# Work moved from VectorE to ScalarE in the first block: normalisations, every second negative branch, two weight casts

## The chip, the core and the metric

The kernel runs on one core of a Trainium2 chip. PE is the matrix engine TensorE, DVE is VectorE, ACT is ScalarE, POOL is GpSimd and SP is SyncE, which issues the transfers. The metric is the device time of one execution in microseconds (us), as the median of several runs.

## The reference

Causal window attention with a distance bias feeds a leaky two-matrix MLP, and that feeds a second MLP. All values are fp32.

```python
scores = scale * q @ k.T                     # 4 batches, 8 heads, 576 rows, 64 wide
scores = where(0 <= rel < 128, scores + bias, -1e9)
x = softmax(scores) @ v                      # as 2304 tokens x 512
h = x @ w_in                                 # 512 x 2048
g = maximum(h, 0) + alpha * minimum(h, 0)    # alpha: one number for each of 2048 columns
x = g @ w_out                                # 2048 x 512
h = x @ w_in2
out = (h * sigmoid(1.702 * h)) @ w_out2
```

## The kernel before

**Numbers in two parts.** Most products are made of a high and a low part: a cast to the rounded type gives the high part (`wh`, `xh`, `gh`), a subtraction the low part (`wl`, `xl`, `gl`), and three matmuls stand for one exact product. The weights come as 64-bit patterns and are turned into fp32 on the chip. There are 32 chunks of 128x512 for the first MLP, two for each of 16 columns of tiles f. A chunk is loaded to `ws`; ACT scales its two halves (`w_scale`, lines 146 and 147); DVE masks the sign (line 151), shifts (156) and adds (161) into `wd`; and `w_split` casts the high part (lines 101 and 102) and subtracts for the low one (106). `HI_DVE` names the chunks whose cast is done by DVE, all others go to ACT. There are four buffers `ws`; the next load is issued when the add of the chunk four places earlier is in the program (`w_ahead`).

**Attention.** An item is one head of one batch, and the first 16 items (n below 16) take a form in full fp32. For each, PE makes scores `s` (line 342), DVE adds the bias and finds the extreme (362), ACT takes the exponential (378), DVE the reciprocal of the sum (386, 387), `a_norm` multiplies by it (396 on ACT, 398 on DVE), PE transposes to `pt` (411), ACT copies `pt` out of PSUM (418) and PE multiplies by v, held in `vz` (432). An item has two tiles here, of 128 and 256 columns. With `"mix"` the first is normalised on DVE and the second on ACT, with `"act"` both on ACT. Items from 16 on split q and k in two parts (lines 315 to 352) in buffers that take the place of the first form's.

**First MLP.** Block k is 256 tokens, which are eight items, so block 0 can start when items 0 to 7 are done. A unit (k, f) has four steps: `m1_h` makes h in one of two PSUM banks (line 493), `m1_n` makes `n = min(h, 0) * alpha` (line 507), `m1_g` makes `g = max(h, 0) + n` (513) and its high part (515), `m1_lo` the low part, and `m1_o`, two units later, accumulates the second product (537). Two units go with one item.

**Order.** A first loop runs items 0 to 9 with the decoding of about 20 chunks. Then come the units of block 0 (k = 0) with items 10 to 17 and the other chunks. The blocks from 1 on have no decoding until the last. Within this program a scheduler that works on a modelled timeline places the instructions of each engine, so that the order of one engine's queue is not that of the text. From the last block of the first MLP on the order of some instructions is pinned.

Of the kernel before, what the change touches and what calls it, by code (L numbers as in the profile page):

```python
# [11 lines left out]
F32 = mybir.dt.float32  # L12
# [3 lines left out]
AF = mybir.ActivationFunctionType  # L16
ALU = mybir.AluOpType
# [4 lines left out]
P = 128  # L22
NF = DFF // P
# [17 lines left out]
         {2: (0, 256, 0), 1: (256, 192, 0), 3: (448, 192, 128), 4: (640, 64, 256)})  # L41
MASKED = 1.0e9 * 256.0

HI_DVE = (0, 2)
NST, NWD = 4, 3
KM = NB1 - 2

# [18 lines left out]
def tile_window_attention__then__two_mlps(  # L66
# [13 lines left out]
    nc = tc.nc  # L80
    usrc = (u0, u1)

    const = ctx.enter_context(tc.tile_pool(name="const", bufs=1))
# [7 lines left out]
    ident = const.tile([P, P], F32, name="ident")  # L91
    relt = const.tile([P, 2 * P], F32, name="relt")
    alph = const.tile([P, NF], F32, name="alph")
    x2d = [dram.tile([P, NC, T1], F32, name=f"x2d{i}") for i in range(NB1)]
    g2d = [
        [dram.tile([P, 2, n], F32, name=f"g2d{j}_{p}") for p in range(NF // 2)] for j, (t, n) in enumerate(BLOCKS)
# [2 lines left out]
    def copy(eng, o, i):  # L99
        if eng == "act":  # L100
            return nc.scalar.copy(o, i)  # L101
        return (nc.vector if eng == "dve" else nc.gpsimd).tensor_copy(o, i)

    def sub(eng, o, a, hi):
        e = nc.vector if eng == "dve" else nc.gpsimd
        return e.tensor_tensor(o, a, hi.bitcast(F32), op=ALU.subtract)  # L106
# [5 lines left out]
    def pin(ins):  # L112
        if pinned:
            tc.keep_in_program_order(ins)
# [49 lines left out]
    def w_split(i):  # L164
# [14 lines left out]
        h, l = wt[layer, f]  # L179
        pin(copy("dve" if i in HI_DVE else "act", h[:, part, :], w))  # L180
        pin(sub("dve", l[:, part, :], w, h[:, part, :]))
# [38 lines left out]
    def w(step, lim=2 * NF):  # L220

        names = ("load", "scale", "sign", "shift", "add", "split")
        i = wdone.get(step, 0)
        if i < min(lim, wdone.get(names[names.index(step) - 1], 0)):
            {"scale": w_scale, "sign": w_sign, "shift": w_shift, "add": w_add, "split": w_split}[step](i)
            wdone[step] = i + 1
# [107 lines left out]
    @stage  # L334
    def a_qk(n, b, u, h, U):
        banks = [ps_a.tile([P, 2, 256], F32, tag="a", name="s") for _ in range(1 + u)]
        places = []
        for i, (c0, rows, kk, keys) in enumerate(U["chunks"]):
            o = banks[i // 2][:rows, i % 2, :]
            if n < FP:  # L340
                raw = raw_of(n)[:D]
                nc.tensor.matmul(
                    o[:, :keys], raw[:, c0 : c0 + rows], raw[:, 256 + kk : 256 + kk + keys], start=True, stop=True
                )
                places.append(o[:, :keys])
                continue
            n_ = max(keys, 192)
            kh, kl = ar["kh"], ar["kl"]
            q = ar["q"][:, c0 - U["q0"] : c0 - U["q0"] + rows]
            ks = kk - U["k0"]  # L350
            nc.tensor.matmul(o[:, :n_], q, kh[:, ks : ks + n_], start=True, stop=False)  # L351
            nc.tensor.matmul(o[:, :n_], q, kl[:, ks : ks + n_], start=False, stop=True)  # L352
            places.append(o[:, :keys])
        st["s", n] = places
# [45 lines left out]
    @stage  # L400
    def a_trans(n, b, u, h, U):
        tt = tts[n % 2]
        banks = [ps_a.tile([P, 512], F32, tag="a", name="pt") for _ in range(1 + u)]
        for i, (c0, rows, kk, keys) in enumerate(U["chunks"]):
            for j in range(kk // P, (kk + keys + P - 1) // P):
                col, nq, oc = PTCOL[u][j]
                bank = 1 if col >= 448 else 0
                dst = col - (0, 448)[bank] + (c0 - U["q0"] - oc)

                src = tt[:, i * 256 + j * P - kk : i * 256 + j * P - kk + P]  # L410
                nc.tensor.transpose(banks[bank][:, dst : dst + P], src, ident)  # L411
        st["t", n] = [(x, c, w) for x, (c, w) in zip(banks, ((0, 384), (448, 256)))]
# [45 lines left out]
    @stage  # L458
    def a_x2(n, b, u, h, U):
        nq = U["nq"]  # L460
        if n < FP:
            return
        x = st.pop(("x", n))
        d0 = (h % 2) * D
        nc.vector.tensor_tensor(xps[d0 : d0 + D, :nq], x[:D, :nq], tb[:, :nq], op=ALU.add)

    @stage
    def a_x3(n, b, u, h, U):
        if h % 2 == 0:
            return  # L470
        nq, c, xp = U["nq"], h // 2, xps
        if n < FP:
            xp = st["x", n]
        t = u * B * UNITS[0]["nq"] + b * nq
        done = 0
        while done < nq:
            r = (t + done) % RING
            w = min(nq - done, RING - r)
            nc.scalar.copy(xh[:, c, r : r + w], xp[:, done : done + w])
            sub("dve", xl[:, c, r : r + w], xp[:, done : done + w], xh[:, c, r : r + w])  # L480
            done += w


    gs, accs = {}, {}

    def m1_h(k, f):
        hi, lo = wt[0, f]
        r = (k * T1) % RING
        n = T1 if k < KM else 2 * T1
        ph = ps_h.tile([P, DM], F32, tag="h", name="h")[:, :n]  # L490
        for c in range(NC):
            for i, (w, x) in enumerate(((hi, xh), (hi, xl), (lo, xh))):
                nc.tensor.matmul(  # L493
                    ph, w[:, 0, c * P : (c + 1) * P], x[:, c, r : r + n],
                    start=(c == 0 and i == 0), stop=(c == NC - 1 and i == 2),
                )
        gs[k, f] = ph

    def m1_tile(k, pool, dt, name):
        if k < KM:  # L500
            return pool.tile([P, T1], dt, tag=name, name=name)
        return p2["n1" if name == "n" else "g1"].tile([P, 2 * T1], dt, tag=name, name=name)

    def m1_n(k, f):
        ph = gs[k, f]
        n = m1_tile(k, gt[0], F32, "n")
        nc.vector.tensor_scalar(n, ph, 0.0, alph[:, f : f + 1], op0=ALU.min, op1=ALU.mult)  # L507
        gs[k, f] = (ph, n)

# [246 lines left out]
    n = H + 2  # L756
# [6 lines left out]
    a_x1(n - 2)  # L763
    a_x2(n - 2)
    a_x3(n - 2)
    at0.close()
    gp[0] = p1.enter_context(tc.tile_pool(name="g", bufs=3, side="right"))
    gt[0] = p1.enter_context(tc.tile_pool(name="gt", bufs=2, side="right"))
# [1 line left out]
    steps = [(k, f) for k in range(KM + 1) for f in range(NF)]  # L770
    for s, (k, f) in enumerate(steps):
        n = H + 2 + s // 2
        norm = "mix" if k == 0 else "act"
        if (k, f) == (KM, 0):
            pinned.append(True)
        dec = k == 0 or k == KM
        lim = min(3 * NF, max(W1, wdone["split"]) + 3) if k else W1

        def wd(*names):
            for x in names if dec else ():  # L780
                w(x, lim)

        m = -1 if n == FP else n - 1
        m1_h(k, f)
        if s % 2 == 0:
            a_trans(m)
            a_qk(n)
            a_pt_hi(m, 0)
            m1_n(k, f)
            wd("sign")  # L790
            m1_g(k, f)
            a_pt_hi(m, 1)
            a_bias(n)
            wd("shift")
            a_pt_lo(m, 0)
            a_pt_lo(m, 1)
            wd("add", "scale")
            w_ahead()
            if n + 1 != FP:
                a_split(n + 1)  # L800
            a_exp(n)
            m1_lo(k, f, "dve")
        else:
            a_av(m)
            a_recip(n)
            a_split_v(n)
            a_load(n + 2)
            a_norm(n, norm)
            m1_n(k, f)
            wd("sign")  # L810
            m1_g(k, f)
            a_x1(n - 1)
            wd("shift", "scale")
            a_x2(n - 1)
            wd("add")
            w_ahead()
            m1_lo(k, f, "dve")
            a_x3(n - 1)
            if n + 1 == FP:
                a_trans(n)  # L820
                a_pt_hi(n, 0)
                a_av(n)
                a_parts()
                a_split(FP)
        if k == 0:
            w("split")
        m1_o(k - (f < LAG), (f - LAG) % NF)
        if n == NI + 1 and s % 2:
            at.close()
            p2["ps"] = ctx.enter_context(tc.tile_pool(name="ps_p", bufs=1, space=PSUM))  # L830
            p2["x", 0] = ctx.enter_context(tc.tile_pool(name="p20", bufs=1))
            pre = ExitStack()
            p2["g1"] = pre.enter_context(tc.tile_pool(name="g1", bufs=3))
            p2["n1"] = pre.enter_context(tc.tile_pool(name="n1", bufs=2))
            w_ahead()
        if k == KM:
            w("split", min(3 * NF, W1 + 2 * (f - 2)))
            if f >= 8 and f % 2 == 0:
                x2_split(0, f // 2 - 4)
            if f >= 6 and f % 2 == 0 and f < 14:  # L840
                x2_load(0, f // 2 - 3)
# [11 lines left out]
    ph = ExitStack()  # L853
# [105 lines left out]
```

## Time and profile before

| | |
|---|---|
| median of 3 runs | 979.54 us (978.63 to 979.56) |
| profiled execution, its own time | 976.72 us |
| its span, first to last instruction | 974.9 us |
| PE busy | 937.9 us, 96% of the span |
| DVE busy | 717.0 us, 74% |
| ACT busy | 561.1 us, 58% |
| POOL busy | 89.1 us, 9% |

The shares are means over stages that differ much: block 0 with the decoding lies in the first 131 us, the rest of the first MLP up to 715 us, the second MLP behind that. An end of a matmul in such a profile is modelled, so the distance between the starts of two matmuls is the better measure of PE's rate.

### The profile page before, as it was taken

The page shows a single profiled execution, that of the slowest core. Times are in us where ns is not written, and L with a number is a line of the kernel's source. Part 1 is how long each engine was busy: PE and PEld are TensorE (multiplying, and loading weights), DVE is VectorE, ACT ScalarE, POOL GpSimd, SP SyncE. Part 2 cuts the span into 40 slices and gives each one's busy share as a digit, 9 for nine tenths or more (in the row PEclk, how much of TensorE's full clock was granted, in tenths as well). Part 3 has the DMA queues.
Part 4 walks back from the last instruction along what each step waited for, and adds up shares of the span by engine and source line. Part 5 has one row for each costly group of instructions (what it writes and reads, how often), then busy time and mean ns, then how long its engine had stood idle before and what let it go on. Part 6 is the DMA issues. An engine that isn't in the chain of part 4 may idle for free.

```text
span 974.9 us, 17672 instructions
## 1 busy us (share of the span) xinstructions
PE 937.9 (96%) x6536; PEld 868.4 (89%) x6536; DVE 717.0 (74%) x1777; ACT 561.1 (58%) x1355; POOL 89.1 (9%) x126
## 2 busy tenths in 40 slices
PE   4889989999999999999999999999999989999997
PEld 2579989999999999999988888888888879999997
DVE  5999957778777777777667863897232798878876
ACT  5987656667877777787633443654232644334333
POOL 1000011112222222222100000000000000000000
PEclk9999999999999999999999999999999999999999
DMA  8655521212212223222022334766322333343323
GB/s 240 197 176 169 179 65 55 77 43 86 88 65 88 66 68 94 78 62 93 2 77 85 109 129 153 234 204 220 120 97 87 142 124 125 131 151 109 131 87 109
DMA packets 43894, 112.43 MB, mean 115 GB/s; under 512 B 5024, under 2 KB 15008, under 8 KB 43808
## 3 DMA queue, kind: packets, MB, share of 16 engines
q1 hardware_dynamic: 43808, 111.31, 35.7%
q8 instruction: 51, 0.84, 0.4%
q14 instruction: 35, 0.29, 0.1%
HBM read 82.98 MB, written 28.31 MB: 114 GB/s over the span
## 4 chain that ended last, share of the span: by engine, by line
PE 82%; DVE 2%; issue 1%; ACT 1%; DMA 0%; DVEq 0%; SPq 0%; ACTq 0%
PE h L583 19%; PE h L493 19%; PE p L650 17%; PE o L537 14%; PE p L537 5%; PE x L444 3%; PE pt L411 3%; PE s L351 1%; PE s L352 1%; ACT oh L101 0%; DMA wd<-x2d 0%; DVE ol L106 0%; DVE gs L624 0%; DVE wl L106 0%; DVE g L597 0%
## 5 line engine op out<-in xcount | busy, mean ns | idle before, releaser
L493 PE MATMUL h<-xh,wh 128*128 128x256 f32 (+1 forms) x512 | 154.3, 304 | 3.4 <-DVE g L513 3.3
L493 PE MATMUL h<-xl,wh 128*128 128x256 f32 (+1 forms) x512 | 157.1, 307 | 0.3 <-DVE xl L106 0.3
L493 PE MATMUL h<-xh,wl 128*128 128x256 f32 (+1 forms) x512 | 155.0, 303 | 0.0
L650 PE MATMUL p<-wh,oh 128*128 128x256 f32 x504 | 136.8, 284 | 1.7 <-ACT oh L101 1.3
L650 PE MATMUL p<-wl,oh 128*128 128x256 f32 x504 | 136.5, 283 | 0.0
L537 PE MATMUL o<-gl,wh 128*128 128x256 f32 x448 | 125.2, 281 | 0.6 <-DVE gl L106 0.6
L537 PE MATMUL o<-gh,wl 128*128 128x256 f32 x448 | 124.6, 280 | 0.0
L537 PE MATMUL o<-gh,wh 128*128 128x256 f32 x448 | 122.7, 280 | 0.0
L650 PE MATMUL p<-wh,ol 128*128 128x256 f32 x504 | 120.4, 283 | 1.9 <-DVE ol L106 1.9
L583 PE MATMUL h<-x2h,wh 128*128 128x512 f32 (+1 forms) x320 | 118.3, 370 | 2.2 <-DVE g L597 2.2
L583 PE MATMUL h<-x2l,wh 128*128 128x512 f32 (+1 forms) x320 | 117.7, 368 | 0.0
L583 PE MATMUL h<-x2h,wl 128*128 128x512 f32 (+1 forms) x320 | 117.7, 368 | 0.0
L597 DVE TENSOR_TENSOR g<-h,sg 128x512 f32<-128x512 f32 (+1 forms) x80 | 50.8, 637 | 76.7 <-ACT sg L593 76.3
L493 PEld LDWEIGHTS h<-xh,wh 128*128 128x128 f32 x512 | 98.2, 193 | 8.6 <-DVE g L513 4.1
L493 PEld LDWEIGHTS h<-xl,wh 128*128 128x128 f32 x512 | 98.6, 193 | 5.2 <-DVE st L387 1.3
L493 PEld LDWEIGHTS h<-xh,wl 128*128 128x128 f32 x512 | 98.8, 193 | 2.9
L593 ACT ACTIVATE sg<-h 128x512 f32<-128x512 f32 (+1 forms) x80 | 44.3, 555 | 98.6 <-PE h L583 98.0
L650 PEld LDWEIGHTS p<-wh,oh 128*128 128x128 f32 x504 | 96.4, 192 | 3.0 <-ACT oh L101 2.9
L507 DVE TENSOR_SCALAR n<-h,alph 128x256 f32<-128x256 f32 (+1 forms) x128 | 65.4, 513 | 43.3 <-PE h L493 42.1
L650 PEld LDWEIGHTS p<-wl,oh 128*128 128x128 f32 x504 | 96.7, 192 | 0.1
L650 PEld LDWEIGHTS p<-wh,ol 128*128 128x128 f32 x504 | 86.8, 192 | 2.7 <-DVE ol L106 2.5
L537 PEld LDWEIGHTS o<-gl,wh 128*128 128x128 f32 x448 | 84.2, 188 | 1.9 <-DVE gl L106 0.8
(105 smaller groups left out, 2234.5 us busy)
## 6 DMA issues: line engine op xcount, KB each, us to landing
ws<-in_w_in_dram SPq DMA_DIRECT2D x32, 512.0 KB, 3.6
ws<-in_w_out_dram SPq DMA_DIRECT2D x32, 512.0 KB, 3.9
raw<-in_u_dram SPq DMA_DIRECT2D x32, 512.0 KB, 3.5
g2d<-g SPq DMA_DIRECT2D x32, 512.0 KB, 3.0
gr<-g2d SPq DMA_DIRECT2D x32, 512.0 KB, 3.3
raw<-in_u_dram SPq DMA_DIRECT2D x16, 320.0 KB, 3.0
wd<-x2d SPq DMA_DIRECT2D x36, 128.0 KB, 3.2
out_dram<-ob SPq DMA_DIRECT2D x16, 256.0 KB, 3.9
```

Of the source, the lines that this page charges most:

```text
L351: nc.tensor.matmul(o[:, :n_], q, kh[:, ks : ks + n_], start=True, stop=False)
L352: nc.tensor.matmul(o[:, :n_], q, kl[:, ks : ks + n_], start=False, stop=True)
L411: nc.tensor.transpose(banks[bank][:, dst : dst + P], src, ident)
L444: nc.tensor.matmul(x[:, oc : oc + nq], v, p[:, col : col + nq], start=(i == 0 and k == 0), stop=(i == len(js) - 1 and k == 1), skip_group_ ...
L493: nc.tensor.matmul(ph, w[:, 0, c * P : (c + 1) * P], x[:, c, r : r + n], start=(c == 0 and i == 0), stop=(c == NC - 1 and i == 2),)
L507: nc.vector.tensor_scalar(n, ph, 0.0, alph[:, f : f + 1], op0=ALU.min, op1=ALU.mult)
L537: nc.tensor.matmul(o, w[:, 1, c * P : (c + 1) * P], g, start=(f == 0 and (k == KM or c % 2 == 0) and i == 0), stop=(f == NF - 1 and i == 2 ...
L583: nc.tensor.matmul(ph[:, :n], w[:, f % 2, c * P : (c + 1) * P], x[:, c, :n], start=(c == 0 and i == 0), stop=(c == NC - 1 and i == 2),)
L593: nc.scalar.activation(sg[:, :n], ph[:, :n], AF.Sigmoid, scale=1.702)
L597: nc.vector.tensor_tensor(g[:, f % 2, :n], ph[:, :n], sg[:, :n], op=ALU.mult)
L650: nc.tensor.matmul(o[:, m, :], g[:, a, m * P : (m + 1) * P], w, start=(p == 0 and m == 0 and i == 0), stop=(p == NF // 2 - 1 and i == 2), ...
```

## The change

Three things move from DVE to ACT, all of them in the first 131 us. In block 0 the negative branch n of every unit with odd f is made by ACT, in two instructions: a relu of -h, and a multiplication by -alpha, which lies in a new tile `nalph`. POOL fills that tile once. In block 0 `a_norm` puts both tiles of an item on ACT. And `HI_DVE` is empty, so that the casts of chunks 0 and 2 go to ACT as well.

```diff
-HI_DVE = (0, 2)
+HI_DVE = ()
...
+    nalph = const.tile([P, NF], F32, name="nalph")
...
     def m1_n(k, f):
         ph = gs[k, f]
         n = m1_tile(k, gt[0], F32, "n")
+        if k == 0 and f % 2:
+
+            nc.scalar.activation(n, ph, AF.Relu, scale=-1.0)
+            nc.scalar.mul(n, n, nalph[:, f : f + 1])
+            gs[k, f] = (ph, n)
+            return
         nc.vector.tensor_scalar(n, ph, 0.0, alph[:, f : f + 1], op0=ALU.min, op1=ALU.mult)
...
     a_x3(n - 2)
+    nc.gpsimd.tensor_scalar(nalph, alph, -1.0, None, op0=ALU.mult)
     at0.close()
...
-        norm = "mix" if k == 0 else "act"
+        norm = "act"
```

The scheduler gives all engines another order from there on; line numbers after the change are up to 8 higher. On DVE, at the first two units of block 0, there stand before (`n` and `g` as above, `tt` the tile of scores, `s` in PSUM):

```order
L507 TENSOR_SCALAR n<-h,alph 128x256 x2
L106 TENSOR_TENSOR wl_569<-wd,wh_568 128x512
L161 ISA wd<-ws,wd 128x1024
L362 ISA tt_145,st_147<-s,relht 128x128
L362 ISA st_147 128x1
L362 ISA tt_145,st_147<-s,relht 128x256
L362 ISA st_147 128x1
L513 SCALAR_TENSOR_TENSOR g<-h,n 128x256
```

After the change the same place on DVE reads:

```order
L514 TENSOR_SCALAR n<-h,alph 128x256
L107 TENSOR_TENSOR wl_570<-wd,wh_569 128x512
L157 SCALAR_TENSOR_TENSOR wd<-wd,ws 128x512
L520 SCALAR_TENSOR_TENSOR g<-h,n 128x256
L152 TENSOR_SCALAR ws<-ws 128x512
L363 ISA tt_146,st_148<-s,relht 128x128
L363 ISA st_148 128x1
L363 ISA tt_146,st_148<-s,relht 128x256
L363 ISA st_148 128x1
L162 ISA wd<-ws,wd 128x1024
```

One of the two n is gone, and the first g stands ahead of the bias of the item, not behind it.

On ACT the place of the second and third odd unit of block 0 reads after the change:

```order
L510 ACTIVATE n<-h 128x256
L102 CAST wh_663<-wd 128x512
L511 ACTIVATE n<-n,nalph 128x256
L147 ACTIVATE wd<-ws 128x512
L102 CAST wh_751<-wd 128x512
L522 CAST gh<-g 128x256
L397 ACTIVATE tt_146<-tt_146,st_148 128x128
L397 ACTIVATE tt_146<-tt_146,st_148 128x256
L148 ACTIVATE ws<-ws 128x512
```

Relu and scaling are parted by other work, and the two normalisations of an item follow each other. Before, the stretch around the same casts on ACT had neither n nor a normalisation of 128 columns:

```order
L515 CAST gh<-g 128x256 x2
L147 ACTIVATE ws<-ws 128x512
L146 ACTIVATE wd<-ws 128x512
L101 CAST wh_661<-wd 128x512
L396 ACTIVATE tt_145<-tt_145,st_147 128x256
L101 CAST wh_661<-wd 128x512
```

On PE, the transposes of an item of block 0 stand after the change on both sides of the next item's scores (`o` is the second product, `raw` holds q and k):

```order
L412 MATMUL pt<-ident,tt_147 128x128
L343 MATMUL s<-raw_144 128x128
L343 MATMUL s<-raw_144 128x256
L412 MATMUL pt<-ident,tt_147 128x128 x2
L544 MATMUL o_755<-gl,wh_976 128x256
```

Before, the three transposes of an item stood together, ahead of the scores:

```order
L411 MATMUL pt<-ident,tt_146 128x128 x3
L342 MATMUL s<-raw_143 128x128
L342 MATMUL s<-raw_143 128x256
L537 MATMUL o_752<-gl,wh_860 128x256
L537 MATMUL o_752<-gh,wl_861 128x256
```

The two transposes that need the second tile moved behind the scores.

## Rows read from the trace of the kernel before

**Rows 1.** Busy time by stage; columns: stretch, its length, engines, clock, DMA share, GB/s

```profile
0.00:20.00 20.00, 6.66 (x17) 4.11 (x18) 10.64 (x33) 10.77 (x25) 2.66 (x14) 1.00 0.79 233
20.00:62.00 42.00, 37.26 (x111) 25.42 (x110) 38.90 (x112) 37.47 (x91) 4.49 (x9) 1.00 0.70 210
62.00:70.30 8.30, 6.39 (x33) 5.64 (x34) 7.64 (x21) 5.77 (x15) 0.30 (x1) 0.80 0.60 168
70.30:118.00 47.70, 47.11 (x371) 44.33 (x371) 47.20 (x125) 33.89 (x77) 1.64 (x4) 1.00 0.52 163
118.00:131.00 13.00, 9.03 (x63) 7.75 (x63) 5.96 (x23) 7.21 (x22) 2.52 (x6) 1.00 0.42 129
131.00:715.00 584.00, 583.08 (x4075) 542.83 (x4075) 417.01 (x1081) 366.29 (x951) 77.53 (x92) 1.00 0.31 98
```

**Rows 2.** Order of time on PE: start, length, instruction, idle time before it

```profile
54.35 0.41 PE L493 MATMUL h<-xh,wl 128*128 128x256 f32 x1
54.56 0.41 PE L493 MATMUL h<-xl,wh 128*128 128x256 f32 x1
...
60.90 0.39 PE L493 MATMUL h<-xl,wh 128*128 128x256 f32 x1 [0.34 <-DVE xl L106]
...
61.13 0.28 PE L493 MATMUL h<-xh,wl 128*128 128x256 f32 x1
61.24 0.28 PE L493 MATMUL h<-xl,wh 128*128 128x256 f32 x1
...
62.18 0.52 PE L411 MATMUL pt<-ident,tt 128*128 128x128 f32 x3 [0.54 <-DVE tt L398]
...
64.85 0.45 PE L432 MATMUL x<-pt,vz 128*128 128x256 f32 x1 [1.30 <-ACT pt L418]
...
66.17 0.39 PE L493 MATMUL h<-xh,wh 128*128 128x256 f32 x1 [0.43 <-DVE g L513]
...
113.89 0.39 PE L537 MATMUL o<-gl,wh 128*128 128x256 f32 x1 [0.56 <-DVE gl L106]
...
127.12 0.33 PE L351 MATMUL s<-kh,q 128*128 128x192 f32 x1 [1.18 <-ACT vp L331]
...
130.73 0.39 PE L493 MATMUL h<-xh,wh 128*128 128x256 f32 x1 [1.97 <-DVE g L513]
```

**Rows 3.** Waits of PE from 58 to 131 us: total, times, longest

```profile
PE x L432 <- ACT pt L418: 2.4, 3, 1.3
...
PE h L493 <- DVE g L513: 2.4, 2, 2.0
```

**Rows 4.** Order of time on ACT, the instruction ahead of a pt copy

```profile
63.67 0.67 ACT L147 ACTIVATE ws<-ws 128x512 int32<-128x512 uint32 x1 [1.15 <-DMA ws<-in_w_out_dram]
```

**Rows 5.** Groups by form, 62 to 118 us: busy us, mean ns, idle before

```profile
L147 ACT ACTIVATE ws<-ws 128x512 int32<-128x512 uint32 x13 | 8.9, 686 | 10.0 <-DMA ws<-in_w_out_dram 5.8 <-DMA ws<-in_w_in_dram 4.2
...
L507 DVE TENSOR_SCALAR n<-h,alph 128x256 f32<-128x256 f32 x15 | 7.0, 474 | 0.0
...
L515 ACT CAST gh<-g 128x256 fp32r<-128x256 f32 x15 | 6.0, 407 | 0.0
...
L396 ACT ACTIVATE tt<-tt,st 128x256 f32<-128x256 f32 x6 | 3.1, 514 | 0.1
...
L398 DVE TENSOR_SCALAR tt<-tt,st 128x128 f32<-128x128 f32 x6 | 1.7, 277 | 0.0
```

**Rows 6.** Line 102, the casts on DVE: duration min/median/max in ns, starts

```profile
L102 DVE CAST wh<-wd x2: 420/422/423, 11.8 to 19.1; 128x512 fp32r<-128x512 f32 x2
```

**Rows 7.** Groups by form on ACT, 0 to 131 us

```profile
L101 ACT CAST wh<-wd 128x512 fp32r<-128x512 f32 x30 | 18.5, 617 | 3.6 <-DVE wd L161 3.5
...
L418 ACT COPY pt<-pt 128x384 f32<-128x384 f32 x16 | 7.5, 472 | 3.8 <-PE pt L411 3.8
...
L378 ACT ACTIVATE tt<-tt,st 128x128 f32<-128x128 f32 x17 | 6.8, 402 | 3.9 <-DVE st L362 3.7
...
L331 ACT CAST vp<-raw 128x128 fp32r<-128x128 f32 x2 | 0.6, 295 | 0.0
```

## The prediction

> **What bounds the kernel now.** I read the busy time by stage first, since the change touches only the first 131 us of a span of 974.9 us [rows 1]. From 131 us to 715 us PE is busy for 583.08 of 584.00 us: what that stretch takes is PE's work alone, and DVE and ACT with 417 and 366 us have room. Nothing the change does to their load there can matter, except through the moment at which the stretch begins. So the question is when block 0 of the first MLP ends, at about 131 us.
>
> Ahead of that three stages differ. From 20 to 62 us, the loop over the first heads, all three engines are near their limit: PE 37.26, DVE 38.90 and ACT 37.47 of 42 us. PE is that busy because it is slow: two matmuls of 256 columns start 0.21 us apart at 54 us, and 0.11 us apart at 61 us [rows 2]. That is the 1.2 GHz level first and the 2.4 GHz level then; the granted clock of the stretch reads 1.00, so for this stage I go by the starts. PE had worked nearly without gaps before it rose.
>
> From 62 to 70.3 us PE idles for 1.91 us (8.30 less 6.39) and its granted clock is 0.80 on the mean. A mean of 0.80 is 3.3 us at half speed, so 1.66 us of PE's work are lost (8.3 x 0.20). Just before it fell, PE had waited four times, and its rows say for what [rows 2]: 0.34 us for xl, 0.54 us for a normalised tile, 1.30 us for a pt copy, 0.43 us for g. In the view of waits from 58 to 131 us [rows 3] g has 2.4 us in two waits, the other of them at 130.7 us, and pt copies have 2.4 us in three. The 1.30 us look like ACT, but the row of ACT [rows 4] shows that the instruction ahead had waited 1.15 us for a weight load. That load could start only when the DVE add of an earlier chunk had freed its buffer. Here PE waits for DVE four times, once by way of a DMA and ACT.
>
> From 70.3 to 118 us PE is busy for 47.11 of 47.70 us and DVE for 47.20. Both are full; PE's one gap there is 0.56 us for gl at 113.9 us [rows 2]. ACT is busy for 33.89 us, and 10.0 us of its idle time between 62 and 118 us stand before one line, waiting for weight loads [rows 5]. From 118 to 131 us PE idles for 3.97 us: the last head of the first form, the switch of the pools, and the first units of block 1.
>
> **The change part by part.** DVE loses 8 multiplications n of 474 ns, 8 normalisations of 277 ns [rows 5] and 2 casts of 422 ns [rows 6]: 3.79 + 2.22 + 0.84 = 6.85 us, all before 131 us.
>
> ACT takes over four kinds. The two casts cost 617 ns there [rows 7], 1.23 us. They fall where DVE had them, at 11.8 and 19.1 us [rows 6], and there ACT is busy for 10.77 of 20 us [rows 1]; this cover hides the first, and the second stands at the edge of the full stage, where it costs nothing or up to 0.62 us. The normalisation of 128 columns has no row on ACT. It lies between 295 ns (a cast of that size without a per-partition operand) and 402 ns (an exponential with two) [rows 7]; I take 400, as it has one: 3.2 us. The scaling by nalph is of the form of the normalisation of 256 columns, 514 ns [rows 5]: 4.1 us. The relu reads PSUM; between the cast of 128x256, 407 ns [rows 5], and the copy of 384 columns out of PSUM, 472 ns [rows 7], I take the first: 3.3 us. In sum ACT gains 11.8 us.
>
> Is there room? From 62 to 118 us ACT is busy for about 39.7 of 56 us (5.77 + 33.89) [rows 1]. Some 7 of the 8 pairs and 6 of the normalisations fall there, 7 x 0.92 + 6 x 0.40 = 8.8 us, which makes 48.5 us or 87%. DVE goes from 54.8 to 49.9 us, 89%. No engine but PE is then full. The order of ACT has no additional table load.
>
> What PE gets. In the 47.7 us where PE is full, a faster DVE gives nothing. What can be won are PE's gaps up to 118 us. By 63 us DVE is ahead by the two casts and one n, 0.84 + 0.47 = 1.3 us. That is as much as the waits for xl, the tile and g together, which are all for DVE (0.34 + 0.54 + 0.43 = 1.31 us): they go. Of the 1.30 us behind the weight load I count half, 0.65: the load starts as much earlier as the add does, but ACT gets a relu and a scaling in the same queue. The 0.56 us for gl goes, since DVE has 5 us in hand by then. Sum 2.5 us. The 1.66 us of the clock I leave out of the sum: whether it falls depends on how the gaps lie. The bounds of this term are 0 (the gaps only move) and 4.8 us (all of 3.2 us of gaps and the clock).
>
> The gaps from 118 to 131 us stay. They are a serial chain (pt copy, the last product with v, the first q and kh of the new form, bias, g) and the order has the same chain in it; what is late next is this chain, which starts as early as PE is done.
>
> What is queued behind the new instructions: behind a relu, which waits for PE, stand on ACT weight scalings, casts wh, gh casts and the pt copy of the head. The two normalisations of a head now follow each other on ACT, so the second half of a tile is ready about 0.4 us later; the order of PE puts the scores of the next head between the first transpose and the other two. That hides it. Without that cover it would be 8 x 0.4 = 3.2 us. The single nalph instruction on POOL stands there ahead of copies of v, and POOL is busy for 4.49 of 42 us from 20 us on and 2.66 of 20 before [rows 1]. On SP only neighbours among the loads swap; the weight loads follow the DVE adds as before.
>
> The profiled execution is 976.72 us for a span of 974.9 us. The three timed runs have a median of 979.54 us, 2.8 us above it; the difference is applied to the median: 979.54 - 2.5 = 977.0 us. A change of 0.2%, 1.96 us, is about what can be told from none.
>
> **The rivals.** *Nothing reaches PE.* The gaps before 70 us belong to the slow, full stage before them, in which PE itself at 1.2 GHz is the pace. DVE then idles where it was full. For it: PE has no gap at all for most of 47.7 us. Against: three of the four waits before 66.2 us name DVE [rows 2]. Time: 979.5 us, between 978 and 981.
>
> *ACT becomes late.* For an odd unit, h now goes through two ACT instructions, 0.92 us in place of 0.47, and through a queue with 87% load. PE's bank of h is free that much later. If PE had no other matmul to run, each of the 8 units would cost 0.45 us, 3.6 us in all: 983.1 us. It decides from the point where an odd unit's g is later than the 12 matmuls that follow its h, 12 x 0.115 = 1.4 us at the spacing of 61 us [rows 2]. For it: PE waits as long for pt copies as for g [rows 3]. Against: ACT's 10 us of waits for loads [rows 5], which the new work can fill. The Trainium skill, ScalarE: Activation LUTs, section Rules for kernel authors, says to put relu, max and mul on VectorE and not on ScalarE. By that rule the time would be this rival's, 983.1 us; the trace agrees in the price of the single instruction, and no run here shows yet what it is worth to take it off an engine that is full.
>
> *The clock goes along.* PE's gaps before 66 us go, and with them the fall of the clock: 1.66 us more, and perhaps the rise near 60 us comes some us earlier in the full stage. Time: 979.5 - 4.8 = 974.7 us, or 973 with a rise 3 us earlier (half of that saved).
>
> **How the numbers follow.** Forecast (977.0, from 975.5 to 978) 0.40; with the clock 0.13; nothing 0.29; ACT late 0.18. The first ends partly above the bound of 977.6, and I give 0.37 of it to faster; with the clock's 0.13 that is 0.50 faster, 0.31 the same, 0.19 slower. The range reaches from 973.0, the lowest case, to 982.0, most of the way into the slower case; about 0.17 lie outside.
>
> **What would show it.** After: DVE below 95% from 70 to 118 us and ACT above 80%; PE's waits for xl, tt and g before 70 us gone; block 1's first scores about 2.5 us before 127.1 us; PE's busy time from there on unchanged. If PE waits for n, g or gl of odd units, or for pt by more than 2.4 us in sum, ACT is late. If DVE idles and the first scores stay at 127 us, nothing reached PE. The forecast is wrong above all if the stage up to 62 us moves: its end then shifts everything.

## The result, and the profile after the change

The kernel after the change takes 990.17 us (median of 4 runs, 986.88 to 990.93) against 979.55 us before: a ratio of 1.0116 with a 95% interval of 1.0098 to 1.0134. It is 10.6 us slower where 2.5 us of gain were forecast, and outside the range. Each ratio here and below is an estimate of its own, without two runs that were slowed far more, and not the quotient of the two medians beside it, from which it can differ by about 0.1%. The profiled execution took 989.47 us with a span of 987.7 us, 12.8 us longer than the one before.

Busy time by stage of the changed kernel, to be held against [rows 1]:

```profile
20.00:62.00 42.00, 34.53 (x102) 23.31 (x101) 38.88 (x110) 37.54 (x92) 3.49 (x8) 1.00 0.70 211
62.00:70.30 8.30, 8.12 (x42) 6.83 (x42) 8.10 (x22) 8.08 (x21) 0.59 (x2) 1.00 0.60 178
70.30:118.00 47.70, 47.48 (x375) 44.92 (x375) 43.92 (x113) 38.20 (x95) 2.18 (x4) 1.00 0.54 171
...
131.00:715.00 584.00, 578.31 (x4014) 537.17 (x4014) 414.20 (x1069) 360.33 (x944) 77.81 (x92) 0.99 0.30 97
```

From 70.3 to 118 us things went about as forecast: DVE falls from 47.20 to 43.92 us, 92% of the stretch, ACT rises from 33.89 to 38.20 us, 80%, and PE stays full. From 20 to 62 us PE is busy for less than before, 34.53 against 37.26 us, of which more below. The surprise is the last row. In 584 us that were PE's alone it is now busy for 578.31 us, and 4,014 matmul records stand there in place of 4,075. No line of code of that stretch was edited.

The waits of PE from 118 to 720 us (total, times, longest):

```profile
PE h L494 <- DVE g L520: 5.8, 5, 2.0
PE h L494 <- DVE n L520: 1.4, 1, 1.4
```

Before, the same stretch had two waits for g and none for n:

```profile
PE h L493 <- DVE g L513: 2.9, 2, 2.0
```

In both kernels the wait of 2.0 us is the start of block 1 ([rows 2], 1.97 us before). The other rows of the changed kernel that begin with such a wait, in order of time:

```profile
189.95 0.38 PE L494 MATMUL h<-xh,wh 128*128 128x256 f32 x1 [1.11 <-DVE g L520]
312.40 0.58 PE L494 MATMUL h<-xh,wh 128*128 128x256 f32 x1 [1.11 <-DVE g L520]
377.81 0.38 PE L494 MATMUL h<-xh,wh 128*128 128x256 f32 x1 [0.55 <-DVE g L520]
443.41 0.39 PE L494 MATMUL h<-xh,wh 128*128 128x256 f32 x1 [1.11 <-DVE g L520]
508.16 0.50 PE L494 MATMUL h<-xh,wh 128*128 128x512 f32 x1 [1.36 <-DVE n L520]
```

They lie at the starts of blocks 2, 4, 5, 6 and 7 of the first MLP. What happens there is seen at block 4, on PE first:

```profile
307.11 0.28 PE L544 MATMUL o<-gh,wl 128*128 128x256 f32 x1
307.23 0.60 PE L412 MATMUL pt<-ident,tt 128*128 128x128 f32 x4
...
308.72 0.50 PE L494 MATMUL h<-xh,wh 128*128 128x256 f32 x2
...
311.01 0.28 PE L445 MATMUL x<-ptl,vp 128*128 128x64 f32 x1
312.40 0.58 PE L494 MATMUL h<-xh,wh 128*128 128x256 f32 x1 [1.11 <-DVE g L520]
312.78 0.41 PE L494 MATMUL h<-xl,wh 128*128 128x256 f32 x1
```

and on DVE and ACT over the same time:

```profile
306.94 0.48 DVE L466 TENSOR_TENSOR xp<-x,tb 64x320 f32<-64x320 f32 x1 [1.83 <-ACT tb L457]
...
309.03 0.49 DVE L107 TENSOR_TENSOR xl<-xp,xh 128x320 fp32r<-128x320 f32 x1
...
310.51 0.47 DVE L514 TENSOR_SCALAR n<-h,alph 128x256 f32<-128x256 f32 x1
...
311.93 0.41 DVE L520 SCALAR_TENSOR_TENSOR g<-h,n 128x256 f32<-128x256 f32 x1
```

```profile
307.24 1.08 ACT L102 COPY xs<-o 128x512 f32<-128x512 f32 x2
308.20 0.47 ACT L480 CAST xh<-xp 128x320 fp32r<-128x320 f32 x1
```

The last of block 3's second products, o, starts at 307.11 us. The last head of block 4 gets its sum xp only at 306.94 us, its xh behind two copies of o, its xl at 309.03. The first products h of block 4 need them; both PSUM banks for h are then taken until n and g have been made, the first g from 311.93 to 312.34. From xp to g's end that is a chain of 5.4 us, and PE has no old o left to fill it with. In the kernel before, the last head's last product with v starts at 298.63 us, and after the change at 305.50 us. Before, PE then goes without a gap from the old block's last o to h of the new block, and from h to the new block's first o:

```profile
308.82 0.28 PE L537 MATMUL o<-gh,wl 128*128 128x256 f32 x1
308.94 0.28 PE L493 MATMUL h<-xh,wh 128*128 128x256 f32 x1
...
311.57 0.28 PE L493 MATMUL h<-xh,wl 128*128 128x256 f32 x1
311.68 0.28 PE L537 MATMUL o<-gh,wh 128*128 128x256 f32 x1
```

The program says why. PE's list of instructions is laid down when the program is built, by the scheduler, and it can be counted: how many matmuls of the old block (h and o) stand behind the last product with v of the last head that the new block needs. These are what PE can run while that head's x, and the first n and g, are made.

| start of block | 2 | 3 | 4 | 5 | 6 | 7 |
|---|---|---|---|---|---|---|
| before | 12 | 38 | 43 | 43 | 43 | 45 |
| after | 12 | 24 | 12 | 24 | 12 | 24 |

At 0.117 us each, 43 matmuls are 5.0 us, about the length of the chain; 12 are 1.4 us. The waits go with the table: before, the one boundary behind 131 us at which PE waits for g is block 2 (0.92 us); after, each 12 has a wait of 1.11 us, and the 24 have none, 0.55 and 1.36 us (the last is block 7, of 512 columns, whose wait is for n and not for g).

How the loss adds up: the first of the copies that close the first MLP starts at 581.75 us before and at 591.98 after, 10.2 us later, though block 1's first scores, at 126.51 us, were 0.6 us earlier. So 10.8 us are lost between. From 150 us to that copy I took the time from each matmul's start to the next and subtracted 0.1165 us per 256 columns. Intervals with more than 0.3 us left over sum to 1.1 us before and to 7.0 after. The smaller ones sum to 24.1 and 29.0 us; 2.4 of these 4.9 us are in the stretch from 300 to 320 us, where behind the stall of block 4 matmuls start 0.21 us apart. Together that is 10.8 us, as it has to be over the same matmuls; where the other 2.5 us of the small intervals come from is not shown. The profile's remaining 2.6 us of 12.8 lie behind the first MLP, where the granted clock falls to 0.70 from 730 to 735 us. Such a fall is in the profiles of after_again (0.66) and x1_casts (0.83 from 725 to 735 us) too and not in that of one_to_act (1.00), so it goes with neither order.

### The profile page after: what moved, and what is told of

Read it like the earlier page. It is cut to its first block, busy times and chain, and to the rows that moved or that the text cites. A ratio compares the mean times of both kernels' runs of the same rounds, so it can differ in the third digit from the quotient of the medians.

```text
span 987.7 us, 17711 instructions
## 1 busy us (share of the span) xinstructions
PE 945.1 (96%) x6536; PEld 873.3 (88%) x6536; DVE 715.1 (72%) x1759; ACT 567.0 (57%) x1381; POOL 89.2 (9%) x127
## 4 chain that ended last, share of the span: by engine, by line
PE 78%; DVE 4%; ACT 2%; DMA 1%; issue 1%; DVEq 0%; SPq 0%; ACTq 0%
PE h L494 18%; PE h L590 18%; PE p L657 17%; PE o L544 13%; PE p L544 4%; PE x L445 3%; PE pt L412 2%; PE s L352 1%; PE s L353 1%; DMA wd<-x2d 1%; DVE n L514 1%; ACT oh L102 0%; DMA g2d<-g 0%; DVE q L318 0%; DVE g L604 0%
## 5 line engine op out<-in xcount | busy, mean ns | idle before, releaser
L514 DVE TENSOR_SCALAR n<-h,alph 128x256 f32<-128x256 f32 (+1 forms) x120 | 61.6, 516 | 33.4 <-PE h L494 31.5
```

## The experiments

*Theory A*: the loss is the order of the unchanged blocks, and one of the edits switches it. *Rival B*: it is ScalarE's added work in block 0, which makes something late that stays late. *Rival C*: the granted clock falls by itself. Each run has the kernel before beside it on the same chip.

**Each edit alone, and the change without one.** The parts are those of the change's diff; x2_norm has only its last edit, x13_casts_neg all but that one.

x2_norm:

```diff
-        norm = "mix" if k == 0 else "act"
+        norm = "act"
```

> The kernel before with the normalisation edit alone (all of block 0's normalisation on ScalarE). Theory A (the loss is in the order that the scheduler gives to the unchanged blocks from 1 on, and this edit alone brings that order): 986 to 992 us, with stalls of 1 to 2 us before the first g of blocks 3 to 7. Rival B (the loss comes from ScalarE's added load in block 0, of which this edit is 8 of some 30 instructions, and goes on as lateness): 980 to 983 us. Rival C (TensorE's granted clock falls somewhere by itself): no forecast by part, 975 to 990.

Measured: 986.10 us against 978.28, ratio 1.0070 (1.0054 to 1.0087). Its waits from 118 to 720 us:

```profile
PE h L493 <- DVE g L513: 5.8, 5, 2.0
...
PE h L493 <- ACT wh L101: 1.1, 1, 1.1
PE h L493 <- DVE n L513: 0.8, 1, 0.8
```

x13_casts_neg (the change's other edits, with the line above as before):

> The change without its normalisation edit: the two casts and the eight negative branches on ScalarE, block 0's first piece still on VectorE. Theory A: the order of blocks 1 on is the order before, so 977 to 980 us (what is left is the local effect, 0 to 2 us of gain). Rival B: the added load on ScalarE is nearly all there, so 986 to 990 us. Rival C: 975 to 990.

Measured: 978.96 us, ratio 1.0001 (0.9989 to 1.0013).

x1_casts:

```diff
-HI_DVE = (0, 2)
+HI_DVE = ()
```

> The kernel before with the two casts of rounded weights on ScalarE alone. Both A and B: within 1 us of 979.5 (order as before, 0.8 us of work moved in the first 20 us).

Measured: 979.89 us, ratio 1.0009 (0.9996 to 1.0022).

x3_neg (the lines of nalph, relu and scaling):

> The kernel before with the eight negative branches of block 0 on ScalarE alone. Theory A: 978 to 980 us, order of blocks 1 on as before. Rival B: this is the largest part of the added ScalarE work (16 instructions), so 984 to 988 us.

Measured: 978.72 us, ratio 0.9999 (0.9985 to 1.0012).

The normalisation alone brings most of the loss; the other two edits together, with 10 of the 18 instructions that leave VectorE, bring nothing. (Why its ratio is a little below that of the runs further down with the same order was not followed up.) B is refuted for them. For the normalisation itself A and B still agree, since it is also eight instructions on ScalarE.

**One instruction.** Of its eight instructions, only the last turns out to switch the order: with that of step f = 15 alone on ScalarE the list of PE has the counts 12, 24, 12, 24, 12, 24; with any one of the other seven alone it keeps 12, 38, 43, 43, 43, 45. So two kernels that differ in the head of one 0.40 us instruction can be compared.

one_to_act and, with 13 in place of 15, one_earlier:

```diff
-        norm = "mix" if k == 0 else "act"
+        norm = "mix" if k == 0 and f != 15 else "act"
```

> The kernel before with one instruction moved: the 128x128 normalisation of the last item of block 0 (step f = 15), 0.40 us, on ScalarE. The scheduler then gives the order of the change to all later blocks. Theory A (the order is the loss): 984 to 989 us, PE's waits before g 5.8 us in 5 as in the change. Rival B (the loss needs ScalarE's added load of block 0): 979.5 within 1 us, since the load is one instruction.

Measured: 987.15 us against 978.46, ratio 1.0098 (1.0082 to 1.0115).

> The kernel before with one instruction moved to ScalarE, the same kind as in one_to_act but of the item of step f = 13 of block 0, one item earlier. The scheduler's order of the later blocks then stays that of before. Theory A (the order is the loss): 977 to 980 us. Rival B (a normalisation on ScalarE in block 0 costs by itself): 986 to 989 us, as one_to_act.

Measured: 977.99 us against 978.76, ratio 0.9999 (0.9984 to 1.0014).

one_back, the change with

```diff
-        norm = "act"
+        norm = "mix" if (k, f) == (0, 15) else "act"
```

> The change with that same one instruction left on VectorE, all the rest of the change in place. The scheduler then gives the order of before. Theory A: 977 to 980 us, the waits before g 2.5 to 2.9 us in 2. Rival B: 988 to 990 us.

Measured: 977.92 us, ratio 1.0001 (0.9990 to 1.0013). The stretch from 131 to 715 us of the three, by one_to_act, one_earlier and one_back:

```profile
131.00:715.00 584.00, 578.94 (x4026) 537.46 (x4025) 414.19 (x1072) 361.17 (x944) 77.77 (x92) 0.99 0.30 97
```

```profile
131.00:715.00 584.00, 582.80 (x4071) 542.37 (x4069) 416.91 (x1078) 366.04 (x951) 77.56 (x92) 1.00 0.31 98
```

```profile
131.00:715.00 584.00, 583.10 (x4066) 542.79 (x4065) 415.71 (x1075) 364.90 (x949) 77.48 (x92) 1.00 0.30 98
```

PE's busy time there is the first column behind the length: 578.94 us with the switched order, 582.80 and 583.10 without. A holds and B falls: the same kind of instruction one head earlier costs nothing, and the change with 17 of its 18 instructions moved takes the time of before.

**Holding the attention.** pin_after and pin_before, the change and the kernel before, each with the same two lines in the loop of the second products:

```diff
+                if 1 <= k < KM and c == 0 and i == 0:
+                    tc.keep_in_program_order(mm)
```

> The whole change, with the first matmul of each unit's second products in blocks 1 to 6 held behind the attention matmuls that the code has in the same step, so that the scheduler can't let attention slip. Attention of blocks 1 on then stands some 24 matmuls (one unit) ahead of its place in the order of before, and the order is the same as with the kernel before so held. Theory A: 974 to 980 us, the waits before g in blocks 1 to 7 gone or under 1.5 us. If attention that far ahead waits for ScalarE or VectorE instead: waits before x or pt of several us, and 980 to 988. Rival B: 988 to 990.

Measured: 981.09 us against 978.46, ratio 1.0034 (1.0017 to 1.0051).

> The kernel before, held in the same manner. Theory A: within 1.5 us of the held change, on either side. Rival B: the held change stays 8 to 11 us behind this one.

Measured: 979.03 us, ratio 1.0014 (0.9996 to 1.0031). The counts are 48, 78, 70, 67, 67, 69 in both. Most of the 10 us is gone, but 981.09 us lies above theory A's range and in the one for attention that waits for ScalarE or VectorE. The held change is 2.1 us behind the held kernel before, not within 1.5, and neither gains. The waits of pin_after from 131 to 720 us show what came instead:

```profile
PE h L494 <- DVE g L520: 1.6, 1, 1.6
PE pt L412 <- ACT tt L397: 1.2, 1, 1.2
...
PE o L544 <- ACT gh L522: 0.5, 1, 0.5
```

The wait for g that is left is the start of block 1; those of blocks 2 to 7 are gone, and pt and o have new ones in block 1, where the products now ask for attention a unit earlier.

**Holding the filler.** hold_after and hold_before do the reverse: they keep o of a block's last two units behind h of the next block's first two.

```diff
-        m1_h(k, f)
+        mm = m1_h(k, f)
...
-        m1_o(k - (f < LAG), (f - LAG) % NF)
+        if f < LAG and k:
+            with tc.issue_after(mm.ins):
+                m1_o(k - 1, f - LAG + NF)
+        else:
+            m1_o(k - (f < LAG), (f - LAG) % NF)
```

> The whole change, with the second products of a block's last two units (24 matmuls) held on TensorE behind the first products of the next block's first two units, for every block boundary: they are then there to run while VectorE and ScalarE make n and g of the new block. Theory A, with the stall at the boundaries as the place of the loss: the waits before g and n of 118 to 720 us fall from 7.2 us to under 1.5, the stretches at the lower clock behind them go too, and the time is 972 to 979 us, below the kernel before. If the stalls are not the loss: 986 to 990. If x of the new block is late in its turn: waits before xh or xl take the place of those before g, and 978 to 984.

Measured: 978.19 us against 978.76, ratio 0.9995 (0.9981 to 1.0010): inside theory A's range, but not shown to be below the kernel before.

> The kernel before with the same hold. Theory A: its two stalls at block boundaries (1.97 and 0.92 us) and the lower clock behind the first go, so 973 to 978 us, within 2 us of the held change. If the hold only moves the wait: 978 to 981.

Measured: 974.88 us, ratio 0.9973 (0.9961 to 0.9986).

> The change itself again, beside the other three. If the order is all of its loss: 985 to 989 us, as one_to_act, 7 to 10 us over before. If its other two edits add to it under that order: 989 to 992 us.

Measured: 987.80 us, ratio 1.0101 (1.0083 to 1.0119), which agrees with one_to_act's ratio: nothing beyond the intervals is left for the other edits to add. Rival C falls too: in all these runs the loss comes with the switched order and goes with it, and after_again has it without the fall of the clock at block 4 that the change's profile has (last section).

The hold takes 9.6 us off the change, and the kernel before with it is the fastest of all, 3.9 us under before by the medians and 2.6 us by the ratio. The counts are 24, 58, 63, 48, 43, 45 for hold_after and 24, 42, 43, 43, 43, 45 for hold_before. hold_before's waits of PE from 131 to 720 us hold no stall at a block's start any more (L584 is the second MLP), and hold_after's one, for xl in block 2:

```profile
PE h L584 <- DVE g L598: 2.1, 2, 1.6
```

```profile
PE h L494 <- DVE xl L107: 0.9, 1, 0.9
```

The two differ by 3.3 us (2.2 by the ratios), more than the 2 us that were expected. In the profiles the first MLP of the held change ends 1.3 us later (the first of its closing copies starts at 581.66 us, not 580.40) and its span is 1.8 us longer; the wait for xl is 0.9 of it. The rest was not settled.

## Why the prediction was wrong

**The step that failed** is its first one: that from 131 us on "nothing the change does to their load there can matter, except through the moment at which the stretch begins". The load did not matter: DVE and ACT have 414 and 360 us of 584 to do there, no more than before. But the order in which the scheduler puts matmuls of old blocks and products with v is made anew for the whole program, and it moved at each block's start. It was there to be read before any run: the two lists of PE differ in the counts above. I looked at the order around the edits alone. No rival held this, so the range ended at 982 on prices of block 0.

**The prices were right.** In the rows of ACT up to 131 us the scaling by nalph measures 519 ns (514 taken), the normalisation 405 (400), the cast 619 (617), and the relu 381, less than the 407 taken:

```profile
L102 ACT CAST wh<-wd 128x512 fp32r<-128x512 f32 x32 | 19.7, 619 | 0.2 <-DVE wd L162 0.2
...
L511 ACT ACTIVATE n<-n,nalph 128x256 f32<-128x256 f32 x8 | 4.2, 519 | 0.1
L510 ACT ACTIVATE n<-h 128x256 f32<-128x256 f32 x8 | 3.0, 381 | 0.3 <-PE h L494 0.2
...
L397 ACT ACTIVATE tt<-tt,st 128x128 f32<-128x128 f32 x7 | 2.8, 405 | 0.5 <-DVE st L388 0.5
```

**The local gain of 2.5 us did not come either.** With the order of before, one_back and x13_casts_neg show 1.0001 with upper and lower ends of 1.0013 and 0.9989; 2.5 us would be 0.9974. Block 1's first scores came 0.6 us earlier, not 2.5. The waits for xl, for the normalised tile and for the g at 66 us are gone as forecast [rows 2, 3], and that for gl fell to 0.2 us. A wait of 0.7 us for st of DVE's bias step is new, and above all PE now waits for xh, as the waits up to 131 us say:

```profile
PE x L433 <- ACT pt L419: 5.7, 7, 1.8
...
PE h L494 <- ACT xh L480: 2.6, 3, 1.5
```

and the order of time on ACT shows the reason: the scaling of a weight, L148, waits for its load, a cast wh follows, and xh stands behind both. The longest wait for xh ends with PE's matmul at 61.70 us.

```profile
60.18 0.70 ACT L148 ACTIVATE ws<-ws 128x512 int32<-128x512 uint32 x1 [0.36 <-DMA ws<-in_w_in_dram]
60.75 0.64 ACT L102 CAST wh<-wd 128x512 fp32r<-128x512 f32 x1
61.26 0.40 ACT L480 CAST xh<-x 128x256 fp32r<-128x256 f32 x1
```

So "ACT becomes late" was right in kind and wrong in place: it was not the odd units' h but xh of the first loop that was late. It goes with the two casts, which the prediction had at nothing or up to 0.62 us. x1_casts, which moves them alone, has PE waiting 2.01 us at this place, and x3_neg, which leaves them on DVE, 0.72:

```profile
63.26 0.79 PE L493 MATMUL h<-xh,wh 128*128 128x256 f32 x2 [2.01 <-ACT xh L479]
```

```profile
58.51 0.50 PE L494 MATMUL h<-xh,wh 128*128 128x256 f32 x2 [0.72 <-ACT xh L480]
```

In the seven profiles with the casts on ACT this wait is 1.39 to 2.06 us, in the seven without it is at most 0.73.

The work did fill ACT's waits for loads: those between 62 and 118 us fell from 10.0 [rows 5] to 5.6 us. The Trainium skill (ScalarE: Activation LUTs, Rules for kernel authors) puts relu and multiplication on VectorE. The trace agrees in the single instruction: relu and scaling take 381 + 519 ns on ACT, n takes 474 ns on DVE [rows 5]. The prediction's rival of a late ACT had 983.1 us; with the order of before the runs show neither that loss nor a gain.

**The clock.** From 62 to 70.3 us the granted clock reads 1.00 after the change and 0.80 before, as in the rival. But the starts contradict it, as they did in the stage ahead. After the change h of 256 columns starts 0.21 us apart up to 64.22 us, and the closer spacing that came at 61.13 us before [rows 2] is first seen from 67.69 us on:

```profile
61.70 0.79 PE L494 MATMUL h<-xh,wh 128*128 128x256 f32 x2 [1.49 <-ACT xh L480]
...
63.80 0.41 PE L494 MATMUL h<-xh,wl 128*128 128x256 f32 x1
64.01 0.41 PE L494 MATMUL h<-xl,wh 128*128 128x256 f32 x1
...
67.69 0.28 PE L494 MATMUL h<-xl,wh 128*128 128x256 f32 x1
67.81 0.28 PE L494 MATMUL h<-xh,wl 128*128 128x256 f32 x1
```

So the fall was gone because the rise itself came later. If PE ran at the lower level from 61.70 to about 66.8 us, half of that, some 2.5 us by this estimate, was lost, against 1.66 us before. The wait for xh of 1.49 us and this difference, 0.8 us, are about the 2.5 us that were to be gained; the first scores show 0.6 us in all. The stage up to 62 us, whose move was named as the likeliest way to be wrong, did move in this respect. Why the rise came later is not shown.

**What is argued and not shown.** Why the scheduler switches at that one instruction is open. It goes by modelled durations, and the last head of block 0 stands directly ahead of the blocks with the repeating order; no run here looked inside it. The switch was shown by the lists, its price by the runs.

## What to carry to other kernels

Where a scheduler lays out the whole program, compare the engines' lists in the stages that were *not* edited as well, above all on the engine that is full: here moving one 0.40 us instruction to another engine cost 8.7 us by the medians, lost up to 400 us later. Count at each boundary between blocks how much old work the bounding engine has left when the new block's last input is made, and hold that filler in place by an explicit order rather than leave it to chance; that alone was worth 0.27% on the unchanged kernel. An edit that is to be judged for itself is to be timed with that order held.

## What the runs showed of the hardware

The same stall need not bring the same clock. Behind PE's wait of 1.11 us at the start of block 4 the change's profile has matmuls 0.21 us apart for about 3 us, the 1.2 GHz level. one_to_act, with a wait of 1.12 us there, shows the fall too, and after_again, the same kernel as the change, with 1.12 us, does not. The granted clock is the number behind PE's busy time, first the change, then after_again:

```profile
312.00:313.00 1.00, 0.60 (x3) 0.58 0.40 154
313.00:314.00 1.00, 1.00 (x6) 0.50 0.07 16
```

```profile
312.00:313.00 1.00, 1.00 (x10) 1.00 0.08 23
313.00:314.00 1.00, 1.00 (x10) 1.00 0.65 66
```

In the change's own profile the waits of 1.11 us at blocks 2 and 6 were not followed by it either: behind them the starts are 0.12 us apart. A stall of 1.1 us can thus cost 1.1 us or, by the 14 starts from 312.78 to 315.69 us, which take 2.91 us where 14 x 0.1165 are 1.63, some 1.3 us more. And a granted clock of 1.00 was no proof of the higher level: it stands over the stretch from 62 to 70.3 us of the change, in which matmuls of 256 columns start 0.21 us apart.
